# Rows of small products shared by scores and foldings, and foldings run in pairs

## The chip, the cores and the metric

The kernel runs on one core of one Trainium2 chip. The metric is the device time of one execution in microseconds (us). Three runs of the kernel before took 1428.11, 1428.58 and 1428.69 us; the median is 1428.58 us.

## The reference

```python
a = exp(phi - max(phi, axis=2)); a = a / (sum(a, axis=2) + 1e-9)      # (8 batches, 8 heads, 576, 32)
k_m = einsum('bhsm,bhsd->bhmd', a, k);  v_m = einsum('bhsm,bhsd->bhmd', a, v)
s = matmul(q, k_m.T) / sqrt(64); s = exp(s - max(s)); attn = s / (sum(s) + 1e-9)
x = matmul(attn, v_m)                       # heads side by side: x is (4608, 512)
g = x @ w_gate; x = (g / (1 + exp(-g)) * (x @ w_val)) @ w_out          # 512 -> 1536 -> 512
h = x @ w_in;  out = where(h > 0, h, exp(min(h, 0)) - 1) @ w_out2      # 512 -> 2048 -> 512
```

`q` and `k` are scaled by 200, the weights arrive in 64 bits, and the large products are done as three passes on a high and a low part (`wh*ah + wh*al + wl*ah`).

## The kernel before, in words

The kernel has three stages. The first (to about 309 us of the profiled execution) does attention and the first four of twelve hidden blocks of the gated layer (`UA = 4`). The second does the other eight blocks, and the third does the last layer. The change is in the first two.

**Folding.** The values are never multiplied by the attention weights alone. For a batch `b` and a pair `p` of hidden blocks, `vw(b, p)` multiplies the memory values `v_m` (`Bs[b].vt`, 64x32 per head) into the weights `WG[p]`: eight products of 64x32 on 512 columns. They land in one PSUM tile of two banks (`[128, 2, 512]`), and ScalarE copies it to the high part (L265) and VectorE subtracts that for the low part (L266). The result `VW[b, p]` is then the weight of the up products of hidden blocks `2p` and `2p+1` in that batch. Tiles of `VW` have four buffers (`vx_p`). `score(hf)` likewise makes eight products of 64x32, on 288 columns, for one half of a batch (L445), which VectorE transposes (L450) and the softmax follows. `together(...)` keeps the products of one call in one row: the first has its usual priority, and all others stand behind it at high priority. All of these are single F32 products that need two passes each, so the trace counts 16 instructions in a row of eight.

**First stage.** The loop over `b` (L593) traces the dense products of batch `b` (`gate1`, `val1`, `down1`), and `tick()` puts between them the tasks in `todo`: `front_tasks(b + 2)` (transposes of `phi`, `kv_mm`, `kv_out`, `kv_T`; five tasks for a batch from 1 on, six for batch 0) and `back_tasks(b + 1)` (scores, softmax, weights). The foldings `vw(b + 1, 0)` and `vw(b + 1, 1)` come last in `todo` (in batch 0 at two places of a list). Up to batch 5 they use the PSUM tile `ps_kv` (named `G2`), which `kv_mm` uses too.

**Second stage.** `units(n, g)` makes for two batches 16 units. A unit is 12 matmuls into a PSUM tile `pg`, SiLU on ScalarE, 12 matmuls into a PSUM tile `pv`, and the product on VectorE (L703). After each second unit `vw2` makes the folding of the pair after next. There are four PSUM tiles of two banks: for `n = 0` units take tiles 0, 1 and 2 in turn and foldings take tile 3. For `n = 1, 2, 3` units and foldings take tiles 0 and 1 in turn (list `turn`), because tiles 2 and 3 hold the sums (`acc`) of the output steps of `n - 1`, which are traced between the units: `down_steps(..., MIXED, ...)`, 14 steps of two halves (`hf`) of 12 matmuls (L286 to L288), seven products of two steps (`j`). Each step's first matmul is ordered behind the last unit's last matmul (`behind`). After a product's second step ScalarE copies its sums out (L729).

**What sets the order.** The framework's planner orders each engine's instructions by the priority of the trace and by its own estimate of when an instruction can start, and `tc.issue_after(i)` puts what its block traces on the engine of `i` behind `i`; other engines' instructions in the block are not ordered by it. So the order of the code is not that of the engines.

Of the kernel before, what the change touches and what calls it, by code (L numbers as in the profile page):

```python
# [8 lines left out]
F32 = mybir.dt.float32  # L9
# [12 lines left out]
KD = DM // 128  # L22
# [16 lines left out]
def attention_moe_moe(ctx: ExitStack, tc: tile.TileContext, qT, phiT, kv, kv4, w1g, w1o, w2, out):  # L39
# [212 lines left out]

    def vw(b, p, pool=None, ps=None):
        t = VW[b, p] = vx_p.tile([128, 2, 2, 512], F32R, tag="vx", name="vw")
        both = ps or pool.tile([128, 2, 512], F32, tag="at", name="pvw")
        ps = [both[:, g] for g in range(2)]

        def head(j, g):
            r, c = slice(64 * g, 64 * g + 64), slice(32 * j, 32 * j + 32)
            return mm(ps[g][c], lhsT=Bs[b].vt[r, j, :], rhs=WG[p][j][r], start=True, stop=True)  # L260

        together([lambda j=j, g=g: head(j, g) for j in reversed(range(KD)) for g in (1, 0)])
        if b >= NEG or p >= UA // 2:
            with tc.high_priority() if pool is None else nullcontext():
                act(out=t[:, 0], in_=both, func=AF.Copy)  # L265
                tt(out=t[:, 1], in0=both, in1=t[:, 0].bitcast(F32), op=ALU.subtract)  # L266
            return
        for g in range(2):
            last["vwh"] = act(out=t[:, 0, g, :], in_=ps[g], func=AF.Copy)
        for g in range(2):  # L270
            mm(ps[g], lhsT=minus, rhs=t[:, 0, g, :], start=False, stop=True, skip_group_check=True)
            last["vwl"] = act(out=t[:, 1, g, :], in_=ps[g], func=AF.Copy)
            if g == 0:
                last["vwl0"] = last["vwl"]
# [10 lines left out]
    def down(ps, w, hs, ms, start, stop, skip=False):  # L285
        mm(ps, lhsT=w[0][:, ms], rhs=hs[0], start=start, stop=False, skip_group_check=skip)  # L286
        mm(ps, lhsT=w[1][:, ms], rhs=hs[0], start=False, stop=False, skip_group_check=skip)  # L287
        mm(ps, lhsT=w[0][:, ms], rhs=hs[1], start=False, stop=stop, skip_group_check=skip)  # L288

# [38 lines left out]
    class Batch:  # L328
# [72 lines left out]
        def kv_out(self):  # L401
            self.kvm = fr_p.tile([128, 2, 2, D], F32, tag="kvm", name="kvm")
            for g in range(2):
                act(out=self.kvm[:, :, g, :], in_=self.kvp[g], func=AF.Copy, scale=self.rs[:, g:g + 1])

# [18 lines left out]

        def score(self, hf):
            q = self.qr.pop(hf)
# [19 lines left out]

            together([lambda j=j, g=g: head(j, g) for j in range(4) for g in (1, 0)])
            t = self.sc = bk_p.tile([128, 2, HS], F32, tag="sc", name="sc", bufs=2)
            for g in range(2):
                nc.vector.transpose(out=t[:, g], in_=ps[g])  # L450
            self.soft(t, t.rearrange("p g (b m) -> p (g b) m", m=M))

        def soft(self, t, x):
# [58 lines left out]
    def back_tasks(b):  # L512
        z, nxt = Bs[b], Bs[b + 1] if 0 < b < B - 1 else None
        yield lambda: z.score(0)
        yield lambda: (z.norm(0), nxt and nxt.load_q(0))
        yield lambda: (z.attn(0))
        yield lambda: (z.score(1), 1 < b < B - 2 and Bs[b + 2].phi())
        yield lambda: (z.norm(1), nxt and nxt.load_q(1))
        yield lambda: (z.attn(1), z.store_at())
# [73 lines left out]
    for b in range(B):  # L593
# [32 lines left out]
        if b == 0:  # L626
            v = list(vw_tasks(1))
            todo += [bk[0], bk[1], v[0], lambda: Bs[2].phi(), bk[2], bk[3], bk[4], v[1], fr[0], fr[1], bk[5]] + fr[2:] + [lambda: Bs[3].phi()]
        else:
            for i in range(max(len(bk), len(fr))):  # L630
                todo += fr[i:i + 1] + bk[i:i + 1]
            if b + 1 < B:
                todo += vw_tasks(b + 1)
        done = [0, 0]
# [54 lines left out]
    MIX = 1000  # L689
    turn = ([3, 0] + [1, 2, 0] * 10 + [1, 0] * MIX)[:32 + MIX]  # L690

# [6 lines left out]
    def unit2(b, u, out):  # L698
# [3 lines left out]
        pv = up2(b, u, 128, "pv")  # L702
        last["h"] = stt(out=out, in0=s, scalar=1.0, in1=pv, op0=ALU.mult, op1=ALU.mult)  # L703

    def vw2(b, p):
        if len(turn) > MIX:
            ps = bank2(3, "pvw")
        else:
            ps = bank2(turn.pop(0), "pvw")
        vw(b, p, ps=ps)  # L710

# [35 lines left out]
    def down_steps(n, g, steps, comb):  # L747
        acc = {}

        def step(j, name, r, k, chain, *dst):  # L750
# [12 lines left out]
            for hf in range(2):  # L763
# [5 lines left out]
                for o, a, b, f in comb.get((name, 2 * j + hf), []):  # L769
                    with tc.issue_after(last["h"].ins):  # L770
                        tt(out=g[o][:, f], in0=g[a][:, f], in1=g[b][:, f], op=ALU.add if (o, a, b) == (2, 2, 3) else ALU.subtract)
                for i, m in [(i, m) for i in range(2) for m in range(2)]:
                    with behind if hf + i + m == 0 else nullcontext():
                        down(acc[chain][m][:, hf], (w[:, i, 0], w[:, i, 1]), (hs[0][:, i], hs[1][:, i]),
                             slice(128 * m, 128 * m + 128), start and j + i == 0, j + i == 2, not start)
# [34 lines left out]

    unit_end = []
    LAG = 1

    def units(n, g):
# [3 lines left out]
        def unit(i, k, u):  # L818
# [7 lines left out]
            if u % 2 == 1:  # L826
                if 8 * n + i + 2 < len(pairs):
                    vw2(*pairs[8 * n + i + 2])
                if i in (5, 7) and n < B // 2 - 1:
# [326 lines left out]
```

## Time and profile before

| | |
|---|---|
| median of three runs | 1428.58 us |
| profiled execution | 1427.93 us, of which the span (first to last instruction) is 1426.2 us |
| TensorE (PE) busy | 1401.3 us, 98% of the span |
| VectorE (DVE) busy | 1136.1 us, 80% |
| ScalarE (ACT) busy | 862.4 us, 60% |
| mean granted TensorE clock | 0.995 |

Matmuls overlap in the pipeline, so a matmul's own duration is longer than its share. What it costs is the distance from one start to the next. In the timeline a merged line (x16) gives the start of the first and the time from there to the end of the last.

### The profile page before, as it was taken

The numbers are of one execution on the slowest core, as the hardware profiler recorded it, in microseconds if no ns is written. First come the engines' busy times: TensorE is split into PE (matmuls) and PEld (weight loads), VectorE is DVE, ScalarE is ACT, GpSimd is POOL, SyncE is SP. The second block draws the span as 40 slices with busy tenths as digits, with TensorE's granted clock in tenths as the row PEclk, the third lists the DMA queues.
The fourth block names the chain that finished last, engine by engine and source line by source line (L and its number), as shares of the span: only waits on it lengthen the run. The fifth ranks groups of instructions, "written<-read, shape, count | busy, mean of one in ns | idle before, by whom it ended". The sixth has DMA issues, their size and how long they took to land.

```text
span 1426.2 us, 23205 instructions
## 1 busy us (share of the span) xinstructions
PE 1401.3 (98%) x9259; PEld 1211.6 (85%) x9259; DVE 1136.1 (80%) x1452; ACT 862.4 (60%) x1254; POOL 44.8 (3%) x73
## 2 busy tenths in 40 slices
PE   6899999999999999999999999999999999999998
PEld 4787889988999999999988888888888888888887
DVE  7988978778798877877988578885889488957884
ACT  5665545544465555555666388557866587548843
POOL 0000000000000000000000000000000000000000
PEclk8999999999999999999999999999999999999999
DMA  9888512664789887888889756766686667566653
GB/s 378 326 298 292 208 72 101 230 233 175 237 251 309 284 240 232 274 241 287 267 291 364 269 188 206 280 214 189 201 282 219 190 202 265 215 210 203 213 201 132
DMA packets 89484, 337.65 MB, mean 237 GB/s; under 512 B 9376, under 2 KB 23712, under 8 KB 70048
## 3 DMA queue, kind: packets, MB, share of 16 engines
q1 hardware_dynamic: 55312, 254.04, 51.6%
q10 hardware_dynamic: 26880, 51.39, 9.8%
q0 software_dynamic: 7184, 30.74, 8.9%
q8 instruction: 73, 1.20, 0.3%
q14 instruction: 35, 0.29, 0.1%
HBM read 251.13 MB, written 85.00 MB: 236 GB/s over the span
## 4 chain that ended last, share of the span: by engine, by line
PE 93%; DVE 3%; ACT 2%; DMA 1%; issue 1%; ACTq 0%; SPq 0%; DVEq 0%
PE pu L877 12%; PE pu L879 12%; PE pu L878 12%; PE pd L877 5%; PE pd L879 5%; PE pd L878 5%; PE acc L288 4%; PE acc L286 4%; PE acc L287 4%; PE pv L281 3%; PE pg L281 3%; PE pv L283 3%; PE pv L282 3%; PE pg L283 3%; PE pg L282 3%; PE pvw L260 3%
## 5 line engine op out<-in xcount | busy, mean ns | idle before, releaser
L878 PE MATMUL pu<-xlo,w 128*128 128x512 f32 x672 | 261.4, 389 | 0.0
L877 PE MATMUL pu<-xhi,w 128*128 128x512 f32 x672 | 261.4, 389 | 0.0
L879 PE MATMUL pu<-xhi,w 128*128 128x512 f32 x672 | 261.4, 389 | 0.0
L906 ACT ACTIVATE xhi<-g 128x1024 fp32r<-128x1024 f32 x120 | 126.5, 1058 | 106.9 <-PE pu L879 64.3
L907 DVE TENSOR_TENSOR xlo<-g,xhi 128x1024 fp32r<-128x1024 f32 x120 | 145.0, 1220 | 40.7 <-ACT xhi L906 40.6
L879 PEld LDWEIGHTS pu<-xhi,w 128*128 128x128 f32 x672 | 126.1, 188 | 26.3
L878 PEld LDWEIGHTS pu<-xlo,w 128*128 128x128 f32 x672 | 126.1, 188 | 26.2
L877 PEld LDWEIGHTS pu<-xhi,w 128*128 128x128 f32 x672 | 126.1, 188 | 26.1
L287 PE MATMUL acc<-hh,ws 128*128 128x288 f32 x448 | 131.7, 296 | 0.0
L286 PE MATMUL acc<-hh,ws 128*128 128x288 f32 x448 | 131.5, 295 | 0.0
L288 PE MATMUL acc<-hl,ws 128*128 128x288 f32 x448 | 128.8, 297 | 0.0
L281 PE MATMUL pv<-at,vw 128*128 128x288 f32 x384 | 115.6, 301 | 2.4 <-DVE s L306 0.7
L281 PE MATMUL pg<-at,vw 128*128 128x288 f32 x384 | 116.7, 304 | 1.1 <-ACT p L579 0.5
L767 ACT ACTIVATE hh<-gh 128x576 fp32r<-128x576 f32 x112 | 76.0, 685 | 68.6 <-PE acc L287 50.8
L282 PE MATMUL pg<-at,vw 128*128 128x288 f32 x384 | 114.1, 297 | 0.9 <-DVE at L488 0.9
L283 PE MATMUL pg<-at,vw 128*128 128x288 f32 x384 | 113.6, 296 | 0.0
L282 PE MATMUL pv<-at,vw 128*128 128x288 f32 x384 | 113.6, 296 | 0.0
L283 PE MATMUL pv<-at,vw 128*128 128x288 f32 x384 | 113.5, 296 | 0.0
L877 PE MATMUL pd<-xhi,w 128*128 128x512 f32 x288 | 112.0, 389 | 0.0
L878 PE MATMUL pd<-xlo,w 128*128 128x512 f32 x288 | 112.0, 389 | 0.0
L879 PE MATMUL pd<-xhi,w 128*128 128x512 f32 x288 | 112.0, 389 | 0.0
L897 DVE SCALAR_TENSOR_TENSOR et<-et 128x1024 f32<-128x1024 f32 x72 | 87.8, 1219 | 28.8 <-ACT et L896 28.8
(161 smaller groups left out, 3226.9 us busy)
## 6 DMA issues: line engine op xcount, KB each, us to landing
w<-dnd SPq DMA_DIRECT2D x64, 1024.0 KB, 4.9
w<-upd SPq DMA_DIRECT2D x40, 1024.0 KB, 5.7
w<-upd SPq DMA_DIRECT2D x32, 768.0 KB, 4.6
ws<-d1d SPq DMA_DIRECT2D x42, 512.0 KB, 4.5
kvr<-kv SPq DMA_DIRECT2D x32, 512.0 KB, 7.5
wr<-w SPq DMA_DIRECT2D x16, 1024.0 KB, 6.3
upd<-uw ACTq DMA_DIRECT2D x32, 512.0 KB, 6.3
dnd<-uw ACTq DMA_DIRECT2D x32, 512.0 KB, 7.9
```

What stands on the lines that cost most here:

```text
L281: mm(ps, lhsT=wh, rhs=ah, start=g == 0, stop=False)
L282: mm(ps, lhsT=wh, rhs=al, start=False, stop=False)
L283: last["pe"] = mm(ps, lhsT=wl, rhs=ah, start=False, stop=g == 1)
L286: mm(ps, lhsT=w[0][:, ms], rhs=hs[0], start=start, stop=False, skip_group_check=skip)
L287: mm(ps, lhsT=w[1][:, ms], rhs=hs[0], start=False, stop=False, skip_group_check=skip)
L288: mm(ps, lhsT=w[0][:, ms], rhs=hs[1], start=False, stop=stop, skip_group_check=skip)
L877: mm(ps, lhsT=w[0], rhs=x[0], start=start, stop=False, skip_group_check=skip)
L878: mm(ps, lhsT=w[0], rhs=x[1], start=False, stop=False, skip_group_check=skip)
L879: last["mm"] = mm(ps, lhsT=w[1], rhs=x[0], start=False, stop=stop, skip_group_check=skip)
L897: stt(out=a, in0=e, scalar=1.0, in1=a, op0=ALU.add, op1=ALU.mult)
L906: last["hi"] = act(out=hi, in_=x, func=AF.Copy)
L907: last["lo"] = tt(out=lo, in0=x, in1=hi.bitcast(F32), op=ALU.subtract)
```

## The change

Scores and foldings: `score(hf, p)` now makes the folding `(b, p)` and its own products in one `together`, the folding first, for every batch but the first. The foldings leave the end of `todo`; `back_tasks` names `p = 0` for the first half and `p = 1` for the second. A new branch gives an order of `todo` for the case that there are six front tasks.

Second stage: `vw2` takes two foldings and makes them in one `together`. For `n = 0` a pair is made after the second unit of an even pair, in the next tile of the turn and in tile 3. For later `n` the two are put on the list `folds`, and the next output step makes them between its halves, in tiles 0 and 1, the first folding in the tile that the last `pv` used and the next unit's `pg` will use.

```diff
+    def vw_calls(b, p, ps):
         def head(j, g):
...
-        together([lambda j=j, g=g: head(j, g) for j in reversed(range(KD)) for g in (1, 0)])
+        return [lambda j=j, g=g: head(j, g) for j in reversed(range(KD)) for g in (1, 0)]
+
+    def vw(b, p, pool=None, ps=None):
+        both = ps or pool.tile([128, 2, 512], F32, tag="at", name="pvw")
+        together(vw_calls(b, p, both))
+        vw_out(b, p, both, pool)
+
+    def vw_out(b, p, both, pool=None):
+        t = VW[b, p] = vx_p.tile([128, 2, 2, 512], F32R, tag="vx", name="vw")
+        ps = [both[:, g] for g in range(2)]
         if b >= NEG or p >= UA // 2:
             with tc.high_priority() if pool is None else nullcontext():
                 act(out=t[:, 0], in_=both, func=AF.Copy)
-                tt(out=t[:, 1], in0=both, in1=t[:, 0].bitcast(F32), op=ALU.subtract)
+                last["g2"] = tt(out=t[:, 1], in0=both, in1=t[:, 0].bitcast(F32), op=ALU.subtract)
...
-        def score(self, hf):
+        def score(self, hf, p=None):
...
-            together([lambda j=j, g=g: head(j, g) for j in range(4) for g in (1, 0)])
+            more = p is not None and G2.tile([128, 2, 512], F32, tag="at", name="pvw")
+            with tc.issue_after(last["g2"].ins) if more else nullcontext():
+                together((vw_calls(self.b, p, more) if more else []) +
+                         [lambda j=j, g=g: head(j, g) for j in range(4) for g in (1, 0)])
             t = self.sc = bk_p.tile([128, 2, HS], F32, tag="sc", name="sc", bufs=2)
             for g in range(2):
                 nc.vector.transpose(out=t[:, g], in_=ps[g])
             self.soft(t, t.rearrange("p g (b m) -> p (g b) m", m=M))
+            if more:
+                vw_out(self.b, p, more, G2)
...
-        yield lambda: z.score(0)
+        yield lambda: z.score(0, 0 if b else None)
...
-        yield lambda: (z.score(1), 1 < b < B - 2 and Bs[b + 2].phi())
+        yield lambda: (z.score(1, 1 if b else None), 1 < b < B - 2 and Bs[b + 2].phi())
...
         if b == 0:
-            v = list(vw_tasks(1))
-            todo += [bk[0], bk[1], v[0], lambda: Bs[2].phi(), bk[2], bk[3], bk[4], v[1], fr[0], fr[1], bk[5]] + fr[2:] + [lambda: Bs[3].phi()]
+            todo += bk[:2] + [lambda: Bs[2].phi()] + bk[2:5] + fr[:2] + bk[5:] + fr[2:] + [lambda: Bs[3].phi()]
+        elif len(fr) == 6 and b < B - 2:
+            todo += [fr[0], bk[0], fr[1], bk[1], fr[2], bk[2], bk[3], fr[3], bk[4], fr[4], bk[5], fr[5]] + bk[6:]
         else:
             for i in range(max(len(bk), len(fr))):
                 todo += fr[i:i + 1] + bk[i:i + 1]
-            if b + 1 < B:
-                todo += vw_tasks(b + 1)
...
-    turn = ([3, 0] + [1, 2, 0] * 10 + [1, 0] * MIX)[:32 + MIX]
+    turn = ([3, 0] + [1, 2, 0] * 12)[:36] + [0, 1] * (MIX // 2)
...
-    def vw2(b, p):
-        if len(turn) > MIX:
-            ps = bank2(3, "pvw")
-        else:
-            ps = bank2(turn.pop(0), "pvw")
-        vw(b, p, ps=ps)
+    def vw2(*of):
+        at = [turn.pop(0), 3] if len(turn) > MIX else [turn.pop(0) for _ in range(3)][1::-1]
+        ps = [bank2(i, "pvw") for i in at]
+        together([c for bp, t in zip(of, ps) for c in vw_calls(*bp, t)])
+        for bp, t in zip(of, ps):
+            vw_out(*bp, t)
...
                 for i, m in [(i, m) for i in range(2) for m in range(2)]:
+                    if hf == 1 and i + m == 0 and folds:
+                        with tc.issue_after(last["acc"].ins), tc.issue_after(last["pv"].ins):
+                            vw2(*folds)
+                        folds.clear()
                     with behind if hf + i + m == 0 else nullcontext():
...
             if u % 2 == 1:
-                if 8 * n + i + 2 < len(pairs):
-                    vw2(*pairs[8 * n + i + 2])
+                if i % 2 == 0 and n == 0:
+                    vw2(*pairs[i + 2:i + 4])
+                elif i % 2 == 0:
+                    folds.extend(pairs[8 * n + i + 2:8 * n + i + 4])
```

`last["acc"]` is the last matmul of `down`, and `last["pv"]` the VectorE product of L703.

## Rows read from the trace of the kernel before

**Rows 1.** The page: busy time of each engine, and the granted clock by slices.
```profile
PE 1401.3 (98%) x9259; PEld 1211.6 (85%) x9259; DVE 1136.1 (80%) x1452; ACT 862.4 (60%) x1254; POOL 44.8 (3%) x73
PEclk8999999999999999999999999999999999999999
```

**Rows 2.** The page: shares of the chain of waits by engine.
```profile
PE 93%; DVE 3%; ACT 2%; DMA 1%; issue 1%; ACTq 0%; SPq 0%; DVEq 0%
```

**Rows 3.** Busy by stretch: us; PE, PEld, DVE, ACT, POOL busy; clock; DMA.
```profile
100.00:150.00 50.00, 48.71 (x554) 40.18 (x553) 45.32 (x88) 29.51 (x67) 0.00 (x0) 1.00 0.71 248
...
265.00:365.00 100.00, 98.58 (x793) 89.78 (x792) 76.30 (x107) 48.25 (x81) 0.69 (x1) 1.00 0.58 202
365.00:475.00 110.00, 109.88 (x886) 101.29 (x892) 94.54 (x122) 61.40 (x92) 7.73 (x10) 1.00 0.87 267
```

**Rows 4.** PE timeline, a folding alone: start, us, line, tiles, shape, count.
```profile
267.95 0.29 PE L283 MATMUL pg<-at,vw 128*128 128x288 f32 x1
268.18 1.09 PE L260 MATMUL pvw<-wg,vt 64*32 64x512 f32 x16
269.19 0.40 PE L281 MATMUL pv<-at,vw 128*128 128x288 f32 x1
269.43 0.29 PE L282 MATMUL pv<-at,vw 128*128 128x288 f32 x1
```

**Rows 5.** PE timeline, scores alone.
```profile
196.68 0.29 PE L288 MATMUL pd<-hl,woh 128*128 128x288 f32 x1
196.91 0.71 PE L445 MATMUL ps_sc<-qr,kT 64*32 64x288 f32 x16
197.55 0.40 PE L281 MATMUL pg<-at,vw 128*128 128x288 f32 x1
197.79 0.30 PE L282 MATMUL pg<-at,vw 128*128 128x288 f32 x1
```

**Rows 6.** PE timeline, scores and a folding that happen to share a row.
```profile
96.44 0.72 PE L445 MATMUL ps_sc<-qr,kT 64*32 64x288 f32 x16
96.95 1.06 PE L260 MATMUL pvw<-wg,vt 64*32 64x512 f32 x16
97.95 0.40 PE L281 MATMUL pg<-at,vw 128*128 128x288 f32 x1
98.19 0.29 PE L282 MATMUL pg<-at,vw 128*128 128x288 f32 x1
```

**Rows 7.** Timeline, end of a unit and half an output step before a folding.
```profile
430.25 0.30 PE L283 MATMUL pv<-at,vw 128*128 128x288 f32 x1
430.38 0.29 PE L286 MATMUL acc<-hh,ws 128*128 128x288 f32 x1
430.58 0.75 DVE L703 SCALAR_TENSOR_TENSOR gh<-s,pv 128x576 f32<-128x576 f32 x1 [2.16 <-PE pv L283]
...
431.85 0.29 PE L288 MATMUL acc<-hl,ws 128*128 128x288 f32 x1
```

**Rows 8.** Timeline, a folding with nothing in the way of its copies.
```profile
462.69 1.09 PE L260 MATMUL pvw<-wg,vt 64*32 64x512 f32 x16
463.89 1.03 ACT L265 ACTIVATE vw<-pvw 128x1024 fp32r<-128x1024 f32 x1 [3.09 <-PE pvw L260]
464.94 1.22 DVE L266 TENSOR_TENSOR vw<-pvw,vw 128x1024 fp32r<-128x1024 f32 x1
```

**Rows 9.** Timeline, the folding whose copies came latest.
```profile
422.35 1.09 PE L260 MATMUL pvw<-wg,vt 64*32 64x512 f32 x16
423.55 1.03 ACT L265 ACTIVATE vw<-pvw 128x1024 fp32r<-128x1024 f32 x1 [1.06 <-PE pvw L260]
423.61 1.22 DVE L132 SCALAR_TENSOR_TENSOR wc<-wr,wc 128x1024 f32<-128x1024 uint32 x1
424.86 1.23 DVE L168 TENSOR_TENSOR uq<-uq,wc 128x1024 f32<-128x1024 f32 x1
426.00 1.22 DVE L266 TENSOR_TENSOR vw<-pvw,vw 128x1024 fp32r<-128x1024 f32 x1
```

More of the change, by code (lines that the diff above doesn't have):

```diff
@@ L249, in attention_moe_moe @@
     raw = {}
[L253 to L256, printed above, removed]
+    def vw_calls(b, p, ps):
         def head(j, g):
             r, c = slice(64 * g, 64 * g + 64), slice(32 * j, 32 * j + 32)
-            return mm(ps[g][c], lhsT=Bs[b].vt[r, j, :], rhs=WG[p][j][r], start=True, stop=True)
-        together([lambda j=j, g=g: head(j, g) for j in reversed(range(KD)) for g in (1, 0)])
+            return mm(ps[:, g][c], lhsT=Bs[b].vt[r, j, :], rhs=WG[p][j][r], start=True, stop=True)
+        return [lambda j=j, g=g: head(j, g) for j in reversed(range(KD)) for g in (1, 0)]
[6 more added lines that the diff above has]
+        ps = [both[:, g] for g in range(2)]
         if b >= NEG or p >= UA // 2:
@@ L271, in vw @@
             mm(ps[g], lhsT=minus, rhs=t[:, 0, g, :], start=False, stop=True, skip_group_check=True)
-            last["vwl"] = act(out=t[:, 1, g, :], in_=ps[g], func=AF.Copy)
+            last["vwl"] = last["g2"] = act(out=t[:, 1, g, :], in_=ps[g], func=AF.Copy)
             if g == 0:
@@ L287, in down @@
         mm(ps, lhsT=w[1][:, ms], rhs=hs[0], start=False, stop=False, skip_group_check=skip)
-        mm(ps, lhsT=w[0][:, ms], rhs=hs[1], start=False, stop=stop, skip_group_check=skip)
+        last["acc"] = mm(ps, lhsT=w[0][:, ms], rhs=hs[1], start=False, stop=stop, skip_group_check=skip)
     def split_h(pool, h, n):
@@ L403, in kv_out @@
             for g in range(2):
-                act(out=self.kvm[:, :, g, :], in_=self.kvp[g], func=AF.Copy, scale=self.rs[:, g:g + 1])
+                last["g2"] = act(out=self.kvm[:, :, g, :], in_=self.kvp[g], func=AF.Copy, scale=self.rs[:, g:g + 1])
         def kv_T(self):
@@ L702, in unit2 @@
         pv = up2(b, u, 128, "pv")
-        last["h"] = stt(out=out, in0=s, scalar=1.0, in1=pv, op0=ALU.mult, op1=ALU.mult)
-    def vw2(b, p):
-        if len(turn) > MIX:
-            ps = bank2(3, "pvw")
-        else:
-            ps = bank2(turn.pop(0), "pvw")
-        vw(b, p, ps=ps)
+        last["pv"] = last["h"] = stt(out=out, in0=s, scalar=1.0, in1=pv, op0=ALU.mult, op1=ALU.mult)
+    def vw2(*of):
[4 more added lines that the diff above has]
+            vw_out(*bp, t)
     held = {}
@@ L811, in attention_moe_moe @@
     unit_end = []
+    folds = []
     LAG = 1
```

## Prediction

> **What bounds the kernel now.** I read the page's engine shares first: TensorE is busy 98% of the span and its granted clock stands at 9 or 10 tenths from the second slice on [rows 1]. The chain of waits says the same: 93% of it is TensorE [rows 2]. So the question is only what the change takes from TensorE's stream and where it makes TensorE wait. The busy time by stretch answers where it waits today. In the stretch of mixed units and output steps it idles 0.12 of 110 us. In the first stage (100 to 150) it idles 1.29 of 50, and from 265 to 365, where the `n = 0` units run, 1.42 of 100 [rows 3]. Then I read the timeline around small rows, since a merged line shows what one costs: the distance from the last dense matmul before it to the second dense matmul behind it, less the two dense steps that would stand there anyway. A dense 288-column matmul takes 0.133 us from start to start (12 of them from 430.25 to 431.85) [rows 7].
>
> **The change part by part.**
>
> *The price of a row.* A folding alone: 267.95 to 269.43 is 1.48 us, less 2 x 0.133 = 1.21 us [rows 4]. 36 foldings stand alone like this, and 35 of them cost 1.21 or 1.22 us. Scores alone: 196.68 to 197.79 is 1.11, less 0.27 = 0.84 us [rows 5]. Where scores and a folding happen to be neighbours, the row runs from 96.44 to 98.19, 1.75 us; with the entry that a row alone has (267.95 to 268.18 is 0.23) and less 0.27 it costs 1.71 [rows 4, 6]. Apart they cost 1.21 + 0.84 = 2.05. So a row has a fixed part of 0.34 to 0.36 us, I take 0.36, which is paid once per row and which sharing saves once: products of one shape follow each other closely, and only entering and leaving them costs.
>
> *How many rows go.* First stage: 14 foldings (batches 1 to 7, two each) join 14 score rows. Two of those pairs are neighbours already (at 54.93 and 96.44), so 12 rows go: 12 x 0.36 = 4.3 us. Second stage: pairs 2 to 31 are 30 foldings, which become 15 rows; 15 go, 4 of them in `n = 0` (1.4 us) and 11 in the mixed stretch (4.0 us). Together 27 x 0.36 = 9.7 us. No DMA is added, and ScalarE and VectorE do the same copies.
>
> *Mixed stretch, the new wait.* Today a folding takes one of the two unit tiles, and the next unit starts in the other one, so its copies have more than a unit's time. Now the pair fills both tiles. The next `pg` needs the tile of the first folding: it stands behind that folding's ScalarE copy and VectorE subtraction. What TensorE has to do meanwhile is fixed: the rest of the row and 12 matmuls. From the row's start that is 1.01 (268.18 to 269.19) plus 0.86 for the second folding (1.21 - 0.36), then 0.24 and 11 x 0.133: `pg` could start at 3.57 [rows 4, 7]. Nothing else can fill a gap: the step behind is ordered after that unit, and all four fold steps (1, 5, 9, 13) are second steps of a product, so the sums must be copied out before the next step begins. The copies end 3.47 after the row's start where nothing is in their way (462.69 to 466.16) [rows 8], and 4.87 after it where VectorE has just begun other work (422.35 to 427.22) [rows 9]. All 23 foldings from 365 to 665 lie between these, their mean is 3.97, and they have high priority there as they will have then. With 0.05 us from a release to the start, `pg` waits for what exceeds 3.52: from 0 to 1.35 us, 0.46 in the mean of the 23. Eleven pairs: 5.0 us, bounds 0 and 15. The second folding is less pressing: `pv` comes 1.6 us later, and its subtraction follows 1.22 behind the first. What is queued behind these copies (SiLU, the high parts of the next step) is needed only after `pg`. The wait for the other side, the first folding's tile that the last `pv` used, is covered: L703 ends 1.08 after that unit's last matmul starts (430.25 to 431.33), and half an output step covers 1.73 [rows 7]; 41 of 45 end by 1.6. Cost nothing.
>
> The Trainium skill, page "TensorEngine Tiling (Array Packing)", section "PSUM Bottleneck", warns that packing small products speeds up TensorE and not the copies out of PSUM, so that these may become the bound. The trace agrees in the mixed stretch (3.97 against 3.57); by the rule the `n = 0` pairs would wait likewise, a result of its own that stands below.
>
> *`n = 0`.* Pairs take the next tile of the turn and tile 3. Two other tiles serve the unit behind it, so the first folding's tile is needed 1.87 + 3.2 = 5.1 us after the row's start, or later if TensorE takes the `pv` of that unit first. Copies there end 4.4 to 6.6 after it in the rows that don't wait for a buffer, so the bounds are 0 and 4 x 1.5 = 6 us. Against it stand the 1.42 us of idle that the present order has there [rows 3]. I take 0 for both together, nearest to the row with 5.1.
>
> *First stage.* The folding goes first in the row, so scores come 0.86 us later, and they now wait for the tile `ps_kv`. The new branch for six front tasks never runs: batches from 1 on have five, and batch 0 has its own list. So in batches 1 to 5 `score(1)` with its folding is traced right behind `kv_mm` and `kv_out` in the same tile, and `issue_after(last["g2"])` orders nothing, as its block has only matmuls and `g2` is on ScalarE or VectorE. The row will therefore wait for `kv_out`, and `kv_mm` for the copies of the folding before it. Dense matmuls fill in behind, because scores of a batch are a whole batch early for the most part. VectorE, busy 45.3 of 50 us in that stretch [rows 3], gets the same work a little later. Bounds: the idle of 1.29 in 50 us could go for four such stretches (minus 4 us at most), or double (plus 4); I take 0.
>
> *Sum.* 1427.93 (profiled execution) - 9.7 + 5.0 = 1423.2. The median of the runs is 0.65 above the profiled one, so 1423.9 us.
>
> **The rivals.**
>
> *The copies are hidden.* The planner sees the tight place in its own estimates and starts the copies on free engines, so that they end at 3.5 as in rows 8. For it: 5 of the 23 do. Against: VectorE is busy 94.5 of 110 us there, with pieces of 1.2 us [rows 3, 9]. Time: 1428.6 - 9.7 = 1418.9.
>
> *The change doesn't do what it says.* Scores and foldings don't form rows in the first stage, since the first folding product starts alone when `ps_kv` comes free and the scores' tile or `q` is not ready. For it: the dead branch. Against: scores have been ready for long at that time. Then 4.3 us of the gain is missing: 1428.6.
>
> *Copies bind at the `n = 0` pairs too* (the rule above): 4 x 0.46 = 1.8 us more, 1425.7. Against it: the third tile.
>
> *Slower: the pair slips behind the half step.* If the last `pv`'s product is late on VectorE, TensorE takes the 12 matmuls first and then the row, and nothing is left to cover the copies: `pg` could start at 1.87 and gets its tile at 4.02, 2.15 us of waiting per pair. All eleven: 23.7 - 9.7 makes 1442.6. The other pairs waiting 0.46, it turns slower than before once three of eleven slip (8 x 0.46 + 3 x 2.15 = 10.1 us). For it: 4 of 45 products end later than 1.73 after the `pv`. Against: the other 41.
>
> **How the numbers follow.** Forecast 0.40, hidden copies 0.24, no rows in the first stage 0.16, `n = 0` bound 0.08, slip 0.12. The forecast's own range is 1420 to 1429: 0.1 to 0.9 us of waiting per pair. What runs of this kernel can tell from no change is about 0.2%, 2.9 us, so faster means below 1425.7. Faster: 0.24 and 0.32 of the forecast's 0.40, 0.56. Same: 0.08 of the forecast, the 0.08 of the third rival and 0.13 of the missing rows, 0.29. Slower: the slip and 0.03 of the missing rows, 0.15. The range for 8 in 10 runs from 1417.5, below the hidden copies by a little idle that goes, to 1430.5, which takes in the missing rows and the slip of up to three or four pairs.
>
> **What would show it.** Timeline: 15 rows of 32 folding matmuls in the second stage and 14 rows with scores and a folding, each shared row 0.36 cheaper than its two parts. Waits from 365 on: `pg` (L281) waiting for VectorE `vw`, about 5 us over eleven pairs; none is the first rival, and a wait of about 2 us right behind a row is the slip. From 265 to 365 TensorE's idle stays near 1.4. Score rows split by dense matmuls would show the second rival. The prediction is wrong if the fixed part isn't saved in rows of 32, or if new waits stand in the first stage.

## The result and the profile after

The changed kernel takes 1449.01 us (median of four runs, 1447.06 to 1451.3) against 1428.34 us for the kernel before beside it (1427.35 to 1428.69). The ratio is 1.0145, 95% interval 1.0128 to 1.0161: 20.7 us slower, where 4.7 us faster was forecast and the range ended at 1430.5. The profiled execution of the changed kernel has a span of 1445.3 us, 19.1 more than before.

The page of the changed kernel (engine shares, granted clock by slices, chain of waits), to be read beside [rows 1, 2]:

```profile
PE 1398.2 (97%) x9259; PEld 1214.7 (84%) x9259; DVE 1138.1 (79%) x1452; ACT 862.0 (60%) x1254; POOL 45.5 (3%) x73
...
PEclk8999999999999999999999999999999999999999
...
PE 81%; DVE 9%; DMA 4%; ACT 3%; issue 2%; ACTq 0%; SPq 0%; DVEq 0%
```

TensorE does slightly less work than before, and the chain that ended last now runs 9% through VectorE, where it was 3%. The same three stretches as in [rows 3]:

```profile
100.00:150.00 50.00, 45.66 (x516) 39.61 (x516) 43.28 (x84) 27.04 (x62) 0.00 (x0) 1.00 0.72 252
265.00:365.00 100.00, 94.34 (x748) 86.16 (x747) 72.17 (x103) 45.75 (x82) 0.69 (x1) 1.00 0.53 187
365.00:475.00 110.00, 107.45 (x868) 100.27 (x867) 93.29 (x121) 59.91 (x89) 6.85 (x8) 1.00 0.85 272
```

TensorE idles in all three: 4.3 us of the first (1.3 before), 5.7 of the second (1.4), 2.5 of the third (0.1). The changed kernel lags here, by up to 11 us at 365, so these stretches hold somewhat earlier work than the same ones before.

The rows themselves cost what the prediction said. A shared row of the first stage and a pair of the second, TensorE's timeline of the changed kernel:

```profile
145.38 0.29 PE L289 MATMUL pv<-at,vw 128*128 128x288 f32 x1
145.60 1.09 PE L257 MATMUL pvw<-wg,vt 64*32 64x512 f32 x16
146.49 0.69 PE L451 MATMUL ps_sc<-qr,kT 64*32 64x288 f32 x16
147.11 0.40 PE L292 MATMUL pd<-hh,woh 128*128 128x288 f32 x1
147.35 0.30 PE L293 MATMUL pd<-hh,wol 128*128 128x288 f32 x1
...
528.75 1.95 PE L257 MATMUL pvw<-wg,vt 64*32 64x512 f32 x32
530.62 0.40 PE L292 MATMUL acc<-hh,ws 128*128 128x288 f32 x1
530.86 0.30 PE L293 MATMUL acc<-hh,ws 128*128 128x288 f32 x1
```

The first: 145.38 to 147.35 less 0.27 is 1.70 us, where 1.21 + 0.84 - 0.36 = 1.69 was said. The second: 530.86 less 528.53 (0.22 before the row, as at 145.38) less 0.27 is 2.06; 2 x 1.21 - 0.36 = 2.06. All 14 rows of scores and a folding stand in the first stage, and 14 of the 15 pairs in the second. One pair of `n = 0` came apart, its foldings start at 334.86 and 336.73.

So the time went into waits. TensorE's waits of the changed kernel by what released them (us in total, times, longest), first from 40 to 320, then from 320 to 750:

```profile
PE pg L287 <- ACT p L590: 3.1, 5, 0.9
PE pv L287 <- DVE s L312: 2.4, 3, 1.6
PE pg L287 <- DVE s L312: 2.3, 2, 1.4
PE ps_kvm L403 <- DVE vw L272: 1.3, 1, 1.3
...
PE pg L287 <- DVE vw L272: 7.9, 5, 3.0
PE pv L287 <- ACT s L711: 1.4, 2, 1.2
```

The kernel before, from 40 to 320, same groups (its L579 is L590 now, L306 is L312):

```profile
PE pd L286 <- ACT p L579: 1.1, 2, 0.9
PE pv L281 <- DVE s L306: 0.3, 1, 0.3
PE pg L281 <- DVE s L306: 0.2, 1, 0.2
```

For the gate product (L312) TensorE now waits 4.7 us there, 0.5 before. For the folded weights (`vw`) it waits 7.9 us from 320 on.

**A ledger from starts.** For the comparisons below I worked one out from the start times of the matmuls. The 4416 dense matmuls of the first two stages come in the same number in every kernel. The 1536th stands at the end of the first stage, 1920 to 4224 is the mixed stretch. Between two of them the time is the dense steps (0.133 us, 0.238 right behind a row), the small rows at the least distance that a row of those contents has in any of the kernels compared, and what is left over: waits, and dense matmuls that start 0.24 instead of 0.133 us apart, at half speed or as the second behind a wait (called half speed below). From 0 to 4224 the changed kernel takes 19.1 us more: rows 9.2 less, their neighbours 0.5 more, waits 25.1 more, half speed 2.9 more (0.2 is rounding). Each kernel's ledger is that of one profiled execution.

### The profile page after: what moved, and what is told of

The parts are those of the page before. It is cut to its first block, busy times and chain, and to the rows that moved or that the text cites. A ratio compares the mean times of both kernels' runs of the same rounds, so it can differ in the third digit from the quotient of the medians.

```text
span 1445.3 us, 23191 instructions
## 1 busy us (share of the span) xinstructions
PE 1398.2 (97%) x9259; PEld 1214.7 (84%) x9259; DVE 1138.1 (79%) x1452; ACT 862.0 (60%) x1254; POOL 45.5 (3%) x73
## 4 chain that ended last, share of the span: by engine, by line
PE 81%; DVE 9%; DMA 4%; ACT 3%; issue 2%; ACTq 0%; SPq 0%; DVEq 0%
PE pu L895 12%; PE pu L896 12%; PE pu L894 12%; PE pd L895 5%; PE pd L894 5%; PE pd L896 5%; PE acc L292 4%; PE acc L293 4%; PE acc L294 3%; PE pg L287 3%; PE pv L287 3%; PE pg L289 3%; PE pg L288 3%; PE pv L289 3%; PE pv L288 3%
## 5 line engine op out<-in xcount | busy, mean ns | idle before, releaser
L287 PE MATMUL pg<-at,vw 128*128 128x288 f32 x384 | 119.3, 311 | 15.8 <-DVE vw L272 7.9
L288 PE MATMUL pg<-at,vw 128*128 128x288 f32 x384 | 114.6, 299 | 1.1 <-DVE at L499 1.1
L289 PE MATMUL pg<-at,vw 128*128 128x288 f32 x384 | 114.0, 297 | 0.0
```

The source lines that it names most:

```text
L287: mm(ps, lhsT=wh, rhs=ah, start=g == 0, stop=False)
L288: mm(ps, lhsT=wh, rhs=al, start=False, stop=False)
L289: last["pe"] = mm(ps, lhsT=wl, rhs=ah, start=False, stop=g == 1)
```

## The experiments

**Which part costs it.** Theory A: there are two separate losses; in the second stage a pair holds both tiles until its copies are out, in the first a folding holds `ps_kv`. Rival B: the first stage alone is the cause, since its delayed attention work makes the second stage's copies late. Two runs put one stage of the kernel before into the changed one.

`e1_stage2_only` (first stage of before; `e2_stage1_only` is the reverse, `vw2` and `turn` of before):

```diff
-        yield lambda: z.score(0, 0 if b else None)
+        yield lambda: z.score(0)
...
+            if b + 1 < B:
+                todo += vw_tasks(b + 1)
```

> The changed second stage with the first stage of before. Theory A (two separate losses: in the second stage a pair holds both unit tiles until its copies are out, in the first a folding holds ps_kv): by the times at which the same dense matmul starts in the two traces, the second stage lost 14 us and the first 5, so 1428 + 14 = 1440 to 1445 us. Rival B (the first stage's delayed attention work lands on VectorE in the second stage and makes its copies late): the second stage alone does what I forecast, -5.4 + 5.0, so 1426 to 1430 us.

Measured: 1440.19 us, ratio 1.0088 (1.0073 to 1.0103), 12.8 us above before.

> The changed first stage with the second stage of before. Theory A: 1428 + 5 = 1431 to 1436 us. Rival B: nearly the whole loss of the change, 1443 to 1449 us. If only the 12 shared rows counted (my forecast): 1424 us.

Measured: 1437.17 us, ratio 1.0068 (1.0053 to 1.0083), 9.8 us above before, 1.2 beyond theory A's range. The two make 22.5 where the whole loses 20.7: two separate losses, as theory A says, and B fails. What the first stage's loss comes from is not shown by this.

`e4_live_branch` lets the dead branch run:

```diff
-        elif len(fr) == 6 and b < B - 2:
+        elif len(fr) == 5 and b < B - 2:
...
```

> The changed kernel with the branch that never runs made live for five front tasks: scores and folding of the second half come before kv_mm and kv_out. Theory A for the first stage (the folding holds ps_kv until a buffer for its copies is free, 13 to 17 us, whichever order stands in todo; now both foldings stand ahead of kv_mm): no gain, 1447 to 1453 us. Rival D (the dead branch is what costs in the first stage): the first stage ends about 5 to 9 us earlier, 1440 to 1444 us.

Measured: 1448.57 us, 1.0145 (1.013 to 1.016). The dead branch is not the cause.

**The mixed stretch.** The ledger of dense matmuls 1920 to 4224, us:

| kernel | stretch | rows (number) | waits | half speed |
|---|---|---|---|---|
| before | 334.7 | 28.5 (23) | 0.6 | 0.2 |
| changed | 342.9 | 23.1 (11) | 11.8 | 2.2 |
| first stage of before (e1) | 345.8 | 23.1 (11) | 11.8 | 5.0 |
| e1, single foldings here (e6) | 333.5 | 27.3 (22) | 0.6 | 0.2 |
| changed, tile free after ScalarE (e3) | 329.2 | 23.1 (11) | 0.3 | 0.0 |
| e1, copies queued first (e8) | 335.9 | 23.1 (11) | 5.4 | 1.3 |
| e1, copies through taken slots (e7) | 352.6 | 23.1 (11) | 19.3 | 4.4 |
| e8, pair earlier, copies by halves (e12) | 352.0 | 23.1 (11) | 17.4 | 4.8 |

In the changed kernel the worst rows are those at 499.49 and 607.73. ScalarE's, VectorE's and TensorE's timeline around the first of them:

```profile
500.06 0.63 ACT L739 ACTIVATE ev<-acc 128x576 f32<-128x576 f32 x1
500.59 1.14 ACT L232 ACTIVATE uw<-uq 128x512 fp32r<-128x512 f32 x2
501.63 1.93 ACT L271 ACTIVATE vw<-pvw 128x1024 fp32r<-128x1024 f32 x2
...
501.22 1.35 DVE L781 TENSOR_TENSOR gh<-gh 128x1152 f32<-128x1152 f32 x1
502.49 1.28 DVE L233 TENSOR_TENSOR uw<-uq,uw 128x512 fp32r<-128x512 f32 x2
503.69 1.35 DVE L781 TENSOR_TENSOR gh<-gh 128x1152 f32<-128x1152 f32 x1
504.96 2.34 DVE L272 TENSOR_TENSOR vw<-pvw,vw 128x1024 fp32r<-128x1024 f32 x2
...
506.23 0.40 PE L287 MATMUL pg<-at,vw 128*128 128x288 f32 x1 [3.00 <-DVE vw L272]
```

The first folding's products are there at 500.58. ScalarE does the output step's sums and two pieces of weight preparation first, and VectorE, to whom the copy comes at 502.6, does 2.3 us of preparation and combinations. The copies of this folding end 6.68 us after the row's start. Those of the eleven in this stretch end 3.66 to 6.68 after it, 4.63 in the mean, where 3.97 had been taken [rows 8, 9].

`e3_tile_free_early` lets VectorE subtract the copy from itself, so the tile is free after ScalarE; the low parts of the second stage's folded weights are left out:

```diff
-                last["g2"] = tt(out=t[:, 1], in0=both, in1=t[:, 0].bitcast(F32), op=ALU.subtract)
+                src = t[:, 0].bitcast(F32) if pool is None else both
+                last["g2"] = tt(out=t[:, 1], in0=src, in1=t[:, 0].bitcast(F32), op=ALU.subtract)
```

> The changed kernel, but in the second stage VectorE subtracts the copy from itself and no longer from the PSUM tile, with the same work on every engine; left out are the low parts of the folded weights there. The tile is free after ScalarE's copy, 2.2 us after the row's start where nothing is ahead of it. Theory A (TensorE waits because VectorE's subtraction holds the tile): most of the 11 us of idle before pg in the mixed stretch goes, 1449 -> 1436 to 1441 us, waits of TensorE for VectorE vw under 1 us. Rival C (the waits come from another place in the queue order, and any pairing brings them): 1446 to 1451 us.

Measured: 1434.19 us, 1.0045 (1.0028 to 1.0061), 14.8 us below the changed kernel. No wait for `vw` is left, and the stretch is 4.3 us shorter than with single foldings (e6): the rows' 4.0 us are there once the wait is gone.

`e8_copies_first` (on e1) traces the pair ahead of the step's combinations and puts these and the background work behind the pair's copies:

```diff
-        for after in last.get("h"), first.get("ex"):
+        for after in last.get("h"), first.get("ex"), held_by.get("a"), held_by.get("d"):
...
+                if hf == 1 and folds:
...
+                        vw2(*folds)
+                    held_by.update(a=last["g2a"], d=last["g2"])
+                    background(*waiting.pop())
...
-                    with tc.issue_after(last["h"].ins):
+                    with tc.issue_after(last["h"].ins), tc.issue_after(held_by["d"].ins) if held_by else nullcontext():
```

> First stage of before, second stage as changed, but the background work and the combinations of that step are queued behind the pair's copies on ScalarE and VectorE. Theory A' (the copies come late because of what stands ahead of them in the two queues, uw, gh and ev): the first folding's copies end 3.5 to 4.0 us after the row's start in nearly all eleven pairs, waits of TensorE fall from 10 to 2 to 5 us, 1440 -> 1428 to 1434 us. Rival F (the copies are slow whatever stands ahead): 1438 to 1442 us.

Measured: 1431.06 us, 1.0018 (1.0009 to 1.0028): 2.7 us above before, where e1 was 12.8. The row that answers to the one at 499.49, ScalarE, VectorE and TensorE, and TensorE's waits from 320 to 750:

```profile
489.66 1.94 ACT L273 ACTIVATE vw<-pvw 128x1024 fp32r<-128x1024 f32 x2
...
490.72 2.36 DVE L274 TENSOR_TENSOR vw<-pvw,vw 128x1024 fp32r<-128x1024 f32 x2 [0.45 <-ACT vw L273]
...
488.47 1.95 PE L259 MATMUL pvw<-wg,vt 64*32 64x512 f32 x32
...
492.05 0.36 PE L289 MATMUL pg<-at,vw 128*128 128x288 f32 x1
...
PE pg L289 <- DVE vw L274: 5.8, 7, 1.2
```

The row begins at 488.47, its first copy ends at 491.95 (+3.48), and `pg` starts without a wait. So what stands ahead of the copies in the two queues makes most of the loss. In four other rows the copies still end 4.1 to 5.0 us after the row's start, and behind three of the eleven only six dense matmuls stand before `pg`, not twelve.

`e7_early_copy` (on e1) copies the first folding raw into the slots of `hh` and `hl` and splits it from there:

```diff
+                    x = [hs_p.tile([128, 512], F32, tag=n, name="vwx") for n in ("hh", "hl")]
+                    for g in range(2):
+                        act(out=x[g], in_=both[:, g], func=AF.Copy)
```

> First stage of before, second stage as changed, but in the mixed stretch the first folding of a pair is copied out in full precision by ScalarE first (into two free slots of the step's high and low parts), and high and low part are made from that copy: the PSUM tile is free 1.2 us earlier and VectorE's queue no longer holds it; ScalarE has 1.0 us more per pair. Theory A: TensorE's waits for VectorE vw go as they did where the subtraction left the tile alone, 1440 -> 1423 to 1428 us. Rival: the extra copies and the taken slots give it back, 1432 us and more.

Measured: 1448.47 us, 1.0138 (1.0123 to 1.0153). `pg` waits only 1.9 us for copies, all of it in `n = 0`, but the output steps wait 15.0 us for `hh` and `hl`, whose slots are taken.

`e12_earlier_halves` (on e8) makes the pair after six matmuls of the first half step, with copies by halves:

```diff
+                    if hf == 0 and i == 1 and m == 0 and folds:
...
+                for g in [slice(0, 2)] if pool else [0, 1]:
+                    last["g2a"] = act(out=t[:, 0, g], in_=both[:, g], func=AF.Copy)
```

> First stage as before; second stage with pairs whose copies stand ahead of the background work (as in the experiment that queued them first, 1431.1 us), and in addition the pair stands after half of the first half step instead of between the two, 0.8 us earlier, and its copies go by halves so that VectorE's first subtraction begins after ScalarE's first half copy. If the wait of pg for the copies is all that is left of the loss in the mixed stretch (5.8 us there): waits of 1 to 2 us and 1425 to 1428. If an earlier pair only moves the wait to pv or to the step's own product: 1430 to 1434.

Measured: 1447.15 us, 1.0132 (1.0116 to 1.0148). `pg` waits 13.0 us in nine places. Behind three of the pairs it comes at once, with no dense matmul as cover, and waits 2.1 to 2.5 us. One of them, TensorE's timeline:

```profile
523.27 1.95 PE L259 MATMUL pvw<-wg,vt 64*32 64x512 f32 x32
527.29 0.37 PE L290 MATMUL pg<-at,vw 128*128 128x288 f32 x1 [2.07 <-DVE vw L275]
```

The halves don't help either: ScalarE's second half starts behind VectorE's first subtraction, and the first folding's copies end here 3.87 us after the row's start, where whole copies ended at 3.48 (e8). So both edits work against it. How much each costs no run parts.

`e6_mixed_single` (on e1) keeps pairs for `n = 0` alone:

```diff
-    turn = ([3, 0] + [1, 2, 0] * 12)[:36] + [0, 1] * (MIX // 2)
+    turn = ([3, 0] + [1, 2, 0] * 12)[:36] + [1, 0] * (MIX // 2)
...
-                    folds.extend(pairs[8 * n + i + 2:8 * n + i + 4])
+                    vw2(pairs[8 * n + i + 2])
```

> First stage of before; pairs only where n = 0; single foldings after each second unit in the mixed stretch, as before. By the times of the same dense matmul in the run with the changed second stage alone, the n = 0 part lost 1.3 us and the mixed part 11: theory A says 1427 to 1430 us. If the pairs of n = 0 are the larger part of the second stage's loss: 1435 us and more. If they only save their rows: 1426 us.

Measured: 1428.87 us, 1.0 (0.9991 to 1.001). Between dense matmuls 1536 and 1920 its waits and half speed are 4.1 us, 2.4 before: what its four shared rows save goes into waits there.

**The first stage.** The ledger up to the 1536th dense matmul, us; "lost" is waits and half speed together:

| kernel | stage | rows | lost | median |
|---|---|---|---|---|
| before | 280.0 | 66.3 | 11.5 | 1428.3 |
| changed here, second stage of before (e2) | 289.1 | 62.3 | 24.5 | 1437.2 |
| e2, five `VW` buffers (e5) | 286.0 | 62.4 | 21.0 | 1436.7 |
| e2, same place, rows apart (e9) | 290.5 | 66.0 | 22.5 | 1438.1 |
| e2, scores first in the row (e10) | 284.0 | 66.9 | 15.2 | 1432.9 |
| e2, one folding shared, one late (e11) | 287.2 | 64.5 | 20.1 | 1434.7 |
| e2, thirteen tasks (e13) | 294.6 | 62.3 | 29.6 | 1443.9 |
| e9, thirteen tasks (e15) | 288.9 | 65.0 | 21.7 | 1436.5 |
| before, eleven tasks (e14) | 292.3 | 66.5 | 23.7 | 1438.3 |
| before, softmax cut (e16) | 282.3 | 67.7 | 12.1 | 1427.7 |
| e2, softmax cut (e17) | 279.7 | 64.4 | 13.2 | 1427.7 |
| e14, softmax cut (e18) | 286.8 | 68.2 | 16.3 | 1432.7 |

One of the longer waits of the changed kernel, VectorE's and TensorE's timeline:

```profile
122.19 0.75 DVE L474 TENSOR_REDUCE smx<-sc 128x18 f32<-128x576 f32 x1
...
123.38 0.42 DVE L459 STREAM_TRANSPOSE sc<-ps_sc 128x288 f32<-128x288 f32 x1
123.72 0.71 DVE L477 TENSOR_TENSOR sc<-sc,smx 128x576 f32<-128x576 f32 x1
124.36 0.47 DVE L459 STREAM_TRANSPOSE sc<-ps_sc 128x288 f32<-128x288 f32 x1
124.75 0.73 DVE L496 STREAM_TRANSPOSE ex<-sc 128x576 f32<-128x576 f32 x1
125.41 0.42 DVE L312 SCALAR_TENSOR_TENSOR s<-s,pg 128x288 f32<-128x288 f32 x1
...
125.88 0.40 PE L287 MATMUL pg<-at,vw 128*128 128x288 f32 x1 [1.37 <-DVE s L312]
```

The gate product (L312), which sets a dense tile free, stands behind two softmaxes' pieces. ScalarE had its input ready at 122.46.

`e5_fifth_buffer` (on e2):

```diff
+        fifth = p < 2 and (2 * b + p) % 5 == 4
+        t = VW[b, p] = (bk_p if fifth else vx_p).tile([128, 2, 2, 512], F32R, tag="vx5" if fifth else "vx", name="vw")
```

> The changed first stage with the second stage of before (1437.2 us), and a ring of five buffers for the folded weights in the first stage instead of four. Theory A (a folding that shares a row with early scores must hold ps_kv until one of four buffers is free, 13 to 17 us in four places, and kv_mm and the next scores stand behind it): a fifth buffer lets each folding go about half a batch earlier, most of the 14 us between forecast and result goes: 1424 to 1431 us. Rival E (the order within the row costs: scores behind the folding, more work at once on VectorE): 1435 to 1438 us.

Measured: 1436.69 us, 1.0061 (1.0044 to 1.0078), within e2's interval. A missing buffer is not the main cause.

`e9_same_place_apart` (on e2), `e10_scores_first` (on e2) and `e11_one_shared_late` (on e2), in this order:

```diff
+        yield lambda: (z.score(0), b and vw(b, 0, G2))
...
+                together([lambda j=j, g=g: head(j, g) for j in range(4) for g in (1, 0)] +
+                         (vw_calls(self.b, p, more) if more else []))
...
+        yield lambda: (z.score(1, 0 if b else None), 1 < b < B - 2 and Bs[b + 2].phi())
...
+                todo += [lambda: vw(b + 1, 1, G2)]
```

> Second stage as before; first stage with the foldings at the changed kernel's place in the order of tasks, but as rows of their own behind each half's scores, not in one row with them. Theory P (the early place alone costs the time: each batch's foldings are worked out before the batch ahead has used its buffers, and their copies and the gate products behind them stand in the queues): about 1437 plus the 12 x 0.36 = 4.3 us of rows that no longer share, 1439 to 1443. Theory S (scores and folding tied into one row cost it: scores wait for the tile ps_kv, and softmax and copies come at the same moment): 1427 to 1432.

Measured: 1438.1 us, 1.0071 (1.0056 to 1.0086). Without sharing 22.5 us are lost, with it 24.5 (e2): sharing is not the main cost.

> Second stage as before; first stage as changed, but in the shared row the eight products of the scores come first and the folding's sixteen behind them, so that the scores no longer stand behind a folding that waits for the tile ps_kv. If the scores' delay by that wait is the cost (1437.2 with folding first): 1427 to 1432, and TensorE's waits from 40 to 318 us fall by some 5 us or more. If the place in the order or the joint burst of softmax and copies on VectorE is the cost: 1435 to 1439, waits as before the edit.

Measured: 1432.9 us, 1.0035 (1.0023 to 1.0047), half way. Only 3 rows still hold scores and a folding, since the folding's tile is not free when the scores start. So it doesn't show what delayed scores cost in a shared row.

> Second stage as before; first stage: the first folding of a batch shares the row of the second half's scores (behind kv_mm in the order), the second folding stands alone at the end of the batch's tasks, where the kernel before had it. One row in two is shared, so at most 6 x 0.36 = 2.2 us can be saved. If the early place (a folding ahead of kv_mm that takes its tile, and a VW buffer long before one comes free) is the cost: 1425 to 1430. If every shared row costs by its burst on VectorE, the loss of the first stage (9.8 us with both) halves: 1431 to 1434.

Measured: 1434.66 us, 1.0043 (1.0027 to 1.0059), a loss of 7.0 us and 0.7 beyond the second theory's range. Its list also has twelve tasks, so the run doesn't part the two.

That led to the pace: the change leaves eleven of thirteen tasks in a batch's list, and `tick()` hands them out evenly. `e13_paced` (on e2) and `e15_apart_paced` (on e9) have the first edit, `e14_late_eleven` (on before) the second:

```diff
+            if b + 1 < B:
+                todo += [lambda: None] * 2
...
-                todo += vw_tasks(b + 1)
+                todo[-2:] = [lambda ts=ts: [t() for t in ts] for ts in zip(todo[-2:], vw_tasks(b + 1))]
```

> Second stage as before; first stage as changed, rows shared, but with two empty tasks in each batch's list where the kernel before had its two foldings. The change takes two of thirteen tasks out of the list, and tasks are handed out evenly over a batch, so all tasks of fronts and backs stand later in the changed order (the last ones by up to 2/13 of a batch, some 5 us). Theory T (this later pace costs the time): the first stage recovers its rows, 1424 to 1430, waits of the first 1536 dense matmuls back to 11 to 14 us of lost time. Theory P (the early place of the foldings costs it, whatever the pace): 1435 to 1439, lost time as with the changed first stage alone (24.5 us, before 11.5).

Measured: 1443.86 us, 1.0102 (1.0083 to 1.0122), above both ranges.

> The kernel before with one edit: its two foldings of a batch are called inside the last two tasks of the batch's list instead of as tasks of their own, so the list has eleven tasks and all of them stand later, as in the changed kernel, while foldings stay late, alone and behind everything else. Theory T (pace): 1433 to 1438. Theory P (place of the foldings): 1426 to 1430.

Measured: 1438.34 us, 1.0072 (1.0053 to 1.0092).

> As the experiment with the foldings at the changed place in rows of their own (1438.1), with two empty tasks in each batch's list, so that the pace is the one of before. Theory T: 1427 to 1431. Theory P: 1436 to 1440.

Measured: 1436.46 us, 1.0056 (1.0039 to 1.0073). Both theories fail as single causes: the place costs with the old pace (15.5 us in e13, 8.1 in e15), the pace costs with the old place (10.0 in e14), and both together cost about what the pace alone does (9.8 in e2, 10.4 in e9). What all have in common is that the order of before is left. e14 shows how one such wait comes about, ScalarE's, VectorE's and TensorE's timeline:

```profile
264.92 1.12 ACT L127 ACTIVATE wg<-wr 128x1024 f32<-128x1024 f32 x1 [2.03 <-DMA wr<-w1g]
...
265.94 0.62 ACT L232 ACTIVATE uw<-uq 128x512 fp32r<-128x512 f32 x1
...
266.59 0.69 DVE L233 TENSOR_TENSOR uw<-uq,uw 128x512 fp32r<-128x512 f32 x1 [2.16 <-ACT uw L232]
...
267.20 0.45 DVE L313 SCALAR_TENSOR_TENSOR h<-s,pv 128x288 f32<-128x288 f32 x1
...
267.70 0.45 PE L286 MATMUL pd<-hh,woh 128*128 128x288 f32 x1 [2.50 <-DVE h L313]
```

A weight conversion (L127) at the head of ScalarE's queue waits 2.0 us for its transfer. A piece of weight preparation (L232) stands behind it, VectorE waits for that piece (L233), and the product that TensorE needs (L313) stands behind it there: TensorE waits 2.50 us. The same wait for this transfer, with 2.7 us lost behind it, stands near 260 in e5, e9 and e11. In the kernel before the conversion waits 1.40 us, and TensorE at most 0.5 near it.

`e16_relieved_before` (on before), `e17_relieved_changed` (on e2) and `e18_relieved_late_eleven` (on e14) lighten VectorE:

```diff
-            nc.vector.tensor_reduce(out=mx, in_=x, op=ALU.max, axis=AX.X)
-            last["sub"] = tt(out=sc, in0=x, in1=mx.to_broadcast([128, 2 * HS // M, M]), op=ALU.subtract)
-            act(out=sc, in_=sc, func=AF.Exp, scale=1.0 / float(D) ** 0.5)
+            last["sub"] = act(out=sc, in_=x, func=AF.Exp, scale=0.01 / float(D) ** 0.5)
...
         def norm(self, hf):
+            return
```

> The kernel before without the softmax's maximum and division in the first stage (the exponent's scale is made small instead): some 3.4 us of VectorE per half batch go, 48 of its 242 busy us from 40 to 318. Theory V (the first stage's order is tight because VectorE's queue is nearly full there): lost time before the first 1536 dense matmuls, 11.5 us in the kernel before, falls a little, 1422 to 1428. Theory O (it is the order of dependent steps, not the load): no change, 1427 to 1430.

Measured: 1427.67 us, 1.0008 (0.9995 to 1.0022).

> The changed first stage with the second stage of before (1437.2), relieved in the same way. Theory V: with VectorE at some 70 instead of 87% the new waits go and the shared rows are worth their 3.9 us: 1 to 4 us below the relieved kernel before. Theory O: the waits stay, 6 to 10 us above the relieved kernel before.

Measured: 1427.66 us, 1.0003 (0.9994 to 1.0012).

> The kernel before with eleven tasks to a batch and foldings alone and late (1438.3), relieved in the same way. Theory V: within 2 us of the relieved kernel before. Theory O: 7 to 11 us above it.

Measured: 1432.67 us, 1.0029 (1.0016 to 1.0043). Busy times from 40 to 318 in e2, and the same in e17:

```profile
40.00:318.00 278.00, 264.70 (x2677) 232.66 (x2675) 227.01 (x421) 152.52 (x333) 0.00 (x0) 0.99 0.60 213
```

```profile
40.00:318.00 278.00, 268.19 (x2743) 239.83 (x2742) 193.60 (x341) 157.67 (x338) 0.00 (x0) 1.00 0.62 219
```

With VectorE at 194 instead of 227 us of 278, the changed order's loss against the order of before falls from 9.8 to 0.0 us, and its lost time from 13.0 more than before's to 1.1 more than the relieved one's. With eleven tasks the loss falls from 10.0 to 5.0. So the softmax's work on VectorE is behind most of the loss of the changed order and half of the loss with eleven tasks. Neither theory's figures held: e17 is not 1 to 4 us below e16 and e18 not within 2, as V said, while O held for e16 alone. The trace of the gate product (L312) points to VectorE's queue: from 40 to 318 it starts 0.98 us in the mean after ScalarE's result is ready in e2, 0.52 before, 0.48 in e17. In e14 it is only 0.64, and the wait for the transfer stands in e17 and e18 too, with 2.8 us lost behind it. The rows' 3.3 us show in the ledger (64.4 against 67.7), not in the medians. Open: the cut also shortens the chain from scores to weights and gives the planner another program to order, which these runs don't part from the load.

No version beat both kernels. e6 equals the kernel before; the others are slower, or leave work out.

## Why the prediction was wrong

- **Price and number of rows:** right. 1.70 and 2.06 us a row, and 28 of the 29 shared rows are there; rows and neighbours are 8.7 us less by the ledger, 9.7 forecast. It was never the question.
- **"Mixed stretch, the new wait", 5.0 us: mis-sized.** The mechanism was right and named the right wait, but it measured 11.2 us more of waits and 2.0 more of half speed (4.8 in e1). The step took the copies' delay from foldings that stood at the end of a unit, and moved them without asking what stands in the two queues at the new place: the sums of the output step, the combinations and the weight preparation. With those behind the copies (e8) the waits are 5.4. The Trainium skill, page "TensorEngine Tiling (Array Packing)", section "PSUM Bottleneck", warned that the copies out of PSUM may become the bound; the trace agrees, 4.63 us of copies against 3.57 of cover, and e3 takes the bound away.
- **"*First stage* ... I take 0", bounds -4 to +4: the step that failed.** It cost 13.0 us of lost time (e2), 12.2 in the changed kernel. It looked at whether the row's products would wait, and took TensorE's idle time as the measure of what could go wrong. The relieved kernels point to VectorE's as the measure, whose 45.3 of 50 us it quoted [rows 3] and passed over with "a little later": without the softmax's work there the same order costs 0.0 us. Whether it is the load or the chain that makes it so stays open. Nor did it see that leaving two tasks out moves all the others.
- **`n = 0`, taken at 0:** measured 1.6 to 2.4 us more waits and half speed against rows that save 1.4, so the third rival had the size (1.8). Its wait, `pg` for `vw`, stands there in e1 and e6 at two pairs each; in the changed kernel the waits are others.
- **Clock, not in the sum:** some of the longest waits in the mixed stretch were followed by a run of matmuls at half speed: 11 in the changed kernel (1.2 us), 37 in e1 (4.0 us).
- **Slip of the pair:** the fear was a wait right behind the row; none is there. The slower side came from another place than the rival named. e12 has such a wait, 2.1 to 2.5 us in three places.
- **Range:** each stage's loss alone lies beyond 1430.5. It was built from the idle time and the spread of the old order, and neither bounds a new order.

## What to carry to other kernels

Where a tuned stage keeps TensorE at 98% with VectorE at 84% (91% in its fullest 50 us), as here, a saving of a third of a microsecond per row is small beside what a changed order costs: seven other orders of this first stage lost 5.2 to 15.5 us, and none gained. For every moved step, list what stands in the queues of the engines that must empty its tile at the new place, not at the old; and where tasks are handed out evenly, count a removed task as a move of all others.

## What was not expected of the hardware

A single wait inside a full stream can be followed by TensorE at half its clock. In e1 `pg` waits 3.00 us up to 496.62 (busy times before, in and after; the number behind the five busy times is the granted clock):

```profile
490.00:496.00 6.00, 3.62 (x44) 2.00 (x40) 6.00 (x8) 4.59 (x7) 0.85 (x1) 0.98 0.99 297
496.50:502.00 5.50, 5.38 (x22) 5.38 (x23) 1.20 (x2) 0.65 (x1) 0.00 (x0) 0.50 0.63 222
503.00:508.00 5.00, 5.00 (x39) 5.00 (x39) 4.69 (x9) 3.17 (x5) 0.00 (x0) 1.00 0.43 130
```

The clock granted is 0.50, the lower of its two levels, and 23 matmuls start 0.24 us apart: 2.5 us on top of the wait. It doesn't follow every such wait: in the changed kernel 11 matmuls were slowed after the wait that ended at 614.46, and none after the equal one that ended at 506.23. Shorter waits stand before it too: in e12 the clock is 0.50 from 479.17 on, behind a wait of 1.79 us that ended at 478.81.
